# Second half of a tuned attention and swish kernel: seven products of halves in place of eight, with sums on VectorE

## The chip, the cores and the metric

The kernel runs on one core of a Trainium2 chip. The core has a matrix engine (TensorE, in the profile PE for matmuls and PEld for the loads of their weights), three engines for elementwise work (VectorE or DVE, ScalarE or ACT, GpSimd or POOL), a queue engine (SyncE or SP), a memory of 128 partitions (SBUF) and eight accumulator banks of 128 x 512 f32 (PSUM). The metric is the device time of one execution in microseconds (us).

## What is computed

Attention of two kinds of heads over 4 sequences of 768 tokens with 8 heads of 64, then, on the 3072 x 512 result, a wide layer with a gate of its own for each of its 2048 columns:

```python
def _moe_ref(x, w_in, w_out, beta) -> np.ndarray:
    h = x @ w_in
    g = h * (1.0 / (1.0 + np.exp(-beta * h)))
    return (g @ w_out).astype(np.float32)
...
    mask = np.where(retr[0, :, 0, 0, None, None], full_mask, stream_mask)
    scores = np.where(mask[None, :, :, :], scores, -1000000000.0)
    scores = scores - np.max(scores, axis=-1, keepdims=True)
    a = np.exp(scores)
    a = a / (np.sum(a, axis=-1, keepdims=True) + 1e-09)
    return np.matmul(a, v).astype(np.float32)
```

Three heads of eight see all earlier tokens (`full_mask`), five see the first 4 tokens and a window of 64 (`stream_mask`). x is 3072 x 512, w_in 512 x 2048, w_out 2048 x 512. The change is in the last product, g @ w_out, called the second part below.

## The kernel before

The tokens are cut into eight chunks of 384 (half a sequence), each of three tiles of 128 tokens. For each chunk the kernel goes through the same steps, named as its tasks are:

- `Tk`, `Tq`, `Ek`, `Eq` (chunks 0 to 2) or `Xk`, `Xq` (later chunks): keys and queries are turned so that the head dimension lies on the partitions, on PE with a copy after it or by a transposing DMA on SP. `KO`, `VO` and `lent` are small copies that put key or value blocks side by side.
- `S`, then `exp`: scores of block after block into a bank (L789), and their exponentials on ACT into the tile es (L795).
- `mask` (L820 to L835): es times a mask on DVE, in place.
- `PV` (L855), `rec`, `x` (L858, L865): es times values on PE, with a column of ones that gives the sum of each row; the reciprocal of it and the product with it on DVE.
- `Tx`, `Ex` or `Xx`: x is turned, on PE or by DMA, into xT.
- `F1`, the first part (L901): for each of 16 blocks of 128 columns of w_in four matmuls of 384 columns into a bank; `th` (L907), a tanh on ACT; `gate` (L909), (tanh + 1) times the bank, on DVE, written in bf16 to the tile gT. With tanh the gate is twice too large, and the factor 0.5 is put in at the end.
- `F2`, the second part (L924): for each tile of 128 tokens 16 matmuls of 512 columns of w_out with gT as weights; `osb` (L936, L938): the bank times 0.5 to SBUF, on ACT or DVE; `st` (L941): the store.

All instructions are recorded as tasks with dependencies, and a planner in the kernel (`Plan`) puts them in an order for every engine when the program is built: it walks through time with a cost for each task, and on PE keeps to the script `STEPS`, in which each letter is the next task of the first part (1), the second part (2) or the scores (S). `SHIFT`, `BIAS` and `FORCE` set priorities and the engine of a task, `ORDER` the order of the first loads on POOL's queue, `SESSIONS` how scores are grouped. The queues run in this order on the chip: what stands behind a waiting instruction on its engine waits too. Loads of q, k, v and the weights go through POOL's queue, transposing DMAs and stores through SP's.

Buffers are rings (`Slots`) that a task takes (`Hold`) and the last reader gives back: eight banks, two tiles gT of a whole chunk, two es tiles, three xT, two lent, four osb, five th. The first loads of chunks 0 to 2 have rings of their own (ld, qkp, qkb), unused after that.

Of the kernel before, what the change touches and what calls it, by code (L numbers as in the profile page):

```python
# [136 lines left out]
class Plan:  # L137
# [177 lines left out]
    def let_go(self, h, at):  # L315
        h.users -= 1
        h.until = max(h.until, at)
        if h.users == 0:
# [16 lines left out]
V_LAG = 8  # L335
PHASE = {3, 6}
WHOLE = set()
ADDED = set()
HEAD_PARTS = 3
SESSIONS = {1: [(4, 1), (2, 3), (3, 2), (2, 3)], 2: [(3, 2), (3, 4)], 3: [(3, 3), (4, 3), (3, 4)], 4: [(2, 3),  # L340
            (4, 3)], 5: [(3, 3), (3, 3), (4, 4)], 6: [(3, 3), (3, 3)], 7: [(3, 3), (3, 3), (4, 4)]}
# [4 lines left out]
BIAS = {"Ek": 3000.0, "Eq": -2400.0, "Ex": 2000.0, "KO": -2600.0, "KOs": 3000.0, "VO": 3000.0, "VOs":  # L346
        2600.0, "castk": -600.0, "castq": 1800.0, "exp": 2800.0, "gate": 2600.0, "mask": 2800.0, "rec":
        -2000.0, "th": 600.0, "x": -1400.0}
SHIFT = {"Ek0": 140.0, "Ek1": -170.0, "Ek2": 120.0, "Eq1": 20.0, "Eq2": 20.0, "Ex0": 120.0, "Ex1": 90.0,
# [6 lines left out]
FORCE = {"Ek0.0": "DVE", "Ek0.1": "DVE", "Ek0.2": "DVE", "Ek1.2": "ACT", "Ek2.0": "DVE", "Eq0.0": "ACT",  # L356
# [3 lines left out]
BY_PRIO = 24000.0  # L360
STEPS = ("12S12211S1111S2211S111111S1211S11211121212111121212111111111111112211122S1211222S2S2"
         "11212S222121121111112212211111S22221212111112121S12221S21111S1111121S222122212122121"
         "112112SS2121S12121111212221112111112211S22111212121122221212111222222222222222222222"
         "22")
# [3 lines left out]
def kernel(  # L368
# [46 lines left out]
    f32_r = ring(4, [128, 2, HT, D], F32, "ld", False)  # L415
    qkb = ring(6, [128, 4, HT, D], BF16, "qkb", False)
    qkp = ring(4, [128, HT, 2, D], BF16, "qkp", False)
# [6 lines left out]
    es_r = ring(2, [128, 75 * 128], BF16, "es")  # L424
    lent_r = ring(2, [128, HALF + 128], BF16, "lent")
    x_r = ring(2, [128, MO, HT, 128], BF16, "x")
    xT_r = ring(3, [128, MO, HALF], BF16, "xT")
    gT_r = ring(2, [128, FO, HALF], BF16, "gT")
    th_r = ring(5, [128, HALF], F32, "th", False)
    osb_r = ring(4, [128, d_model], F32, "osb", False)  # L430
    rec_r = ring(4, [128, HT, 2, 1], F32, "rec", False)
    w_in_sb = sb([128, MO, d_ff], BF16, "w_in_sb")
    w_out_sb = sb([128, FO, d_model], BF16, "w_out_sb")
    beta_h = sb([128, FO], F32, "beta_h")
# [6 lines left out]
    A7 = sb([128, 5, 128], BF16, "A7")  # L441
    Ac = sb([128, 5, 128], BF16, "Ac")
# [52 lines left out]
    def less(out, in_):  # L495
        nc.vector.tensor_scalar(out=out, in0=in_, scalar1=-1.0, scalar2=30000.0, op0=ALU.add, op1=ALU.mult)

    t_ac = ops("DVE", 100, [lambda: less(Ac[:, 0:3:2], Mc[:, None, :].to_broadcast([128, 2, 128]))], "adds",
               [t_mc, ops("DVE", 160, [lambda: nc.vector.memset(Ac, 0.0)], "adds", prio=-260)], prio=-240)
    t_as = ops("DVE", 100, [lambda: less(A7[:, 0:3], M7[:, 0:3]), lambda: nc.vector.tensor_copy(out=A7[:, 3:5], in_=A7[:, 1:3])], "adds", [t_m, t_ms, t_m2], prio=-240)  # L500
# [4 lines left out]
    for i, vx in enumerate(V_r.names + VO_r.names):  # L505
        t_ones[id(vx)] = ops("DVE", 24, [lambda vx=vx: nc.vector.memset(vx[:, :, :, D:DE], 1.0)], "ones", prio=-250 + i)
# [87 lines left out]
    EH = {c: Hold(es_r) for c in range(NC)}  # L594
# [75 lines left out]
    GH = {c: Hold(gT_r) for c in range(NC)}  # L670
# [73 lines left out]
    def session(c, parts, prio, lane):  # L744
# [18 lines left out]

        by_pe = c == 0 and WHERE[c][heads[0]][1] in ADDED
        add = []
        if by_pe:
            def put():
                for a, lo, part, bank in work:
                    h = part[0][0]
                    second = SIDE[c, a][0] + lo != PLACE[c, h][0]  # L770
                    m = (Ac[:, 1:4] if second else Ac[:, 0:3]) if retr[h] else (A7[:, 3:5] if second else A7[:, 0:3])
                    m = m.rearrange("p k j -> p (k j)")
                    nc.tensor.matmul(bank.buf[:, 0:m.shape[1]], ident, m, start=True, stop=False)
            add = [t_ac, t_as, t_id]

        def go(_):
            if by_pe:
                put()
            todo = []
            for s in range(2):  # L780
                at = 0
                for a, lo, part, bank in work:
                    if a == s:
                        for h, kk, i, n, place in runs_of(part):
                            todo.append((at, a, h, kk, i, n, place, bank, place + n == len(part)))
                            at += n
            for _, a, h, kk, i, n, place, bank, ends in sorted(todo, key=lambda x: x[:2]):
                of = LH[c].buf[half(a)] if kk[0][0] == "lent" else QH[c].buf[half(a), WHERE[c][h][1]]
                nc.tensor.matmul(bank.buf[:, place * 128:(place + n) * 128], kk[1](), of[:, i * 128:(i + n) * 128], start=not by_pe, stop=not by_pe or ends)  # L789
        occ = max(time) / 2.4 + 2.0 * count + (sum(time) / 2.4 + 140.0 if by_pe else 0.0)  # L790
        t = P.add(f"S{c}.{parts[0][1]}", [("PE", occ, occ + 166)], deps + add, prio, go, take=[w[3] for w in work] + [EH[c]], drop=drops, mode=64, lane=lane)
# [9 lines left out]
    def masks_and_products(c, pairs):  # L801
# [3 lines left out]
        for h in range(H):  # L805
            at, lst = PLACE[c, h]
            if c == 0 and WHERE[c][h][1] in ADDED:
                made[h] = []
                continue
# [80 lines left out]
    def first_part(c, t_beta):  # L890
        F1[c] = []
        late = []
        for fi in range(FO):
# [10 lines left out]
            if fi == HEAD_PARTS - 1 or not HEAD_PARTS:  # L904
# [5 lines left out]
                out=GH[c].buf[:, fi, :], in0=th.buf, scalar=1.0, in1=bank.buf[:, 0:HALF], op0=ALU.add, op1=ALU.mult), take=[GH[c]], drop=[bank, th])  # L910
# [188 lines left out]
```

## Time and profile before

| what | us |
|---|---|
| three runs: lowest, median, highest | 223.81, 225.12, 226.45 |
| the profiled execution, its own time | 223.37 |
| its span, from the first to the last instruction | 221.6 |
| PE busy with first part (L901, 384 columns, 512 matmuls) | 88.6 |
| PE busy with second part (L924, 512 columns, 348 records) | 82.9 |
| DVE busy with gates (L909, 128 of them) | 68.4 |
| DVE with evictions of 512 columns (L938, 13 of them) | 9.0 |
| ACT busy with tanh (L907, 128) | 73.5 |

The granted TensorE clock is 1.00 all the way. The span is what the engines' instructions take, the run's own time includes 1.8 us around it. The busy times of PE count each matmul to its modelled end, so they overlap; what one matmul costs in a row of them is read from starts. A few records are missing (348 of 368 matmuls of 512 columns are there).

### The profile page before, as it was taken

To read this page: it belongs to the slowest core of one execution; us is meant where nothing else is said; L and a number is where in the kernel's file an instruction comes from. 1 tells how busy PE (TensorE), PEld (TensorE's weight loads), DVE (VectorE), ACT (ScalarE), POOL (GpSimd) and SP (SyncE) were. 2 spreads that over 40 slices of the span, in tenths; PEclk is the share of its full clock that TensorE was granted. 3 is DMA by queue.
4 is the path that set the end of the run, shared out by engine and by line. 5 is a ranking of instruction groups with operands and counts; after the bars stand their busy time and mean duration, and the time that the engine had idled before them with its cause. 6 is when DMAs were issued, how large, how long until landed. Compare 5 with 4: busy or idle time off the path is not lost.

```text
span 221.6 us, 5127 instructions
## 1 busy us (share of the span) xinstructions
PE 213.6 (96%) x1927; PEld 125.4 (57%) x1947; DVE 147.1 (66%) x362; ACT 146.9 (66%) x283; POOL 97.7 (44%) x158
## 2 busy tenths in 40 slices
PE   7998999999999999999999999999999999999994
PEld 3665547647665545656655554655565655556553
DVE  6997866978787346568965475766856883338621
ACT  3898964669786777736867687358888886128500
POOL 8996237888598996099759600200000000000000
PEclk9999999999999999999999999999999999999999
DMA  6999999999999999979999942424012101140012
GB/s 166 167 144 206 206 190 190 187 134 211 140 145 141 123 185 193 166 106 181 155 158 144 166 71 74 114 55 133 0 44 53 39 0 47 38 155 23 3 47 96
DMA packets 95673, 26.57 MB, mean 120 GB/s; under 512 B 87184, under 2 KB 92704, under 8 KB 95648
## 3 DMA queue, kind: packets, MB, share of 16 engines
q0 software_dynamic: 66144, 13.24, 75.9%
q1 hardware_dynamic: 28784, 12.53, 27.1%
q10 hardware_dynamic: 720, 0.47, 0.7%
q8 instruction: 15, 0.25, 0.5%
q14 instruction: 10, 0.08, 0.1%
HBM read 27.27 MB, written 6.29 MB: 151 GB/s over the span
## 4 chain that ended last, share of the span: by engine, by line
PE 81%; DMA 10%; POOL 3%; DVE 2%; issue 1%; SPq 1%
PE bank L924 35%; PE bank L901 34%; DMA w_out_sb<-in_moe_w_out_dram 7%; PE bank L855 6%; PE bank L789 5%; DMA xT<-x 2%; DMA ld<-in_k_dram 2%; POOL w_in_sb L566 1%; SPq L883 1%; POOL KO L447 1%; PE bank L612 1%; POOL qkb L554 1%; PE bank L877 1%; PE bank L609 0%; DVE es L835 0%
## 5 line engine op out<-in xcount | busy, mean ns | idle before, releaser
L907 ACT ACTIVATE th<-bank,beta_h 128x384 f32<-128x384 f32 x128 | 73.5, 583 | 25.6 <-PE bank L901 19.2
L901 PE MATMUL bank<-xT,w_in_sb 128*128 128x384 bf16 x512 | 88.6, 327 | 1.0 <-ACT es L795 0.7
L924 PE MATMUL bank<-w_out_sb,gT 128*128 128x512 bf16 (+2 forms) x396 | 86.4, 363 | 1.5 <-issue 0.5
L909 DVE SCALAR_TENSOR_TENSOR gT<-th,bank 128x384 bf16<-128x384 f32 x128 | 68.4, 551 | 16.8 <-ACT th L907 10.3
L795 ACT ACTIVATE es<-bank 128x512 bf16<-128x512 f32 (+3 forms) x129 | 62.0, 587 | 20.2 <-PE bank L789 18.7
L901 PEld LDWEIGHTS <-w_in_sb 128*128 128x128 bf16 x512 | 49.2, 98 | 35.3 <-DMA w_in_sb<-in_moe_w_in_dram 1.2
L924 PEld LDWEIGHTS <-gT 128*128 128x128 bf16 x416 | 37.8, 98 | 39.1 <-issue 0.8
L835 DVE TENSOR_TENSOR es<-es,M 128x768 bf16<-128x768 bf16 (+1 forms) x35 | 18.5, 544 | 11.1 <-ACT es L795 11.1
L582 POOL DMA_DIRECT2D row<-in_k_dram x30 | 22.6, 771 | 4.1 <-DMA w_out_sb<-in_moe_w_out_dram 1.7
L938 DVE TENSOR_SCALAR osb<-bank 128x512 f32<-128x512 f32 (+2 forms) x15 | 9.7, 646 | 22.1 <-PE bank L924 21.6
L582 POOL DMA_DIRECT2D row<-in_q_dram x30 | 22.4, 785 | 0.2
L561 POOL DMA_DIRECT2D VX<-in_v_dram x24 | 21.5, 931 | 2.0 <-DMA w_in_sb<-in_moe_w_in_dram 1.7
L789 PE MATMUL bank<-QT,KT 64*128 64x128 bf16 (+2 forms) x273 | 19.4, 241 | 0.3 <-DVE QT L447 0.2
L855 PEld LDWEIGHTS <-es 128*128 128x128 bf16 x472 | 16.8, 97 | 3.7 <-DVE es L822 0.2
L855 PE MATMUL bank<-VX,es 128*128 128x65 bf16 x392 | 18.0, 193 | 0.2
L936 ACT ACTIVATE osb<-bank 128x512 f32<-128x512 f32 (+1 forms) x11 | 6.2, 568 | 18.0 <-PE bank L924 18.0
L865 DVE TENSOR_TENSOR x<-bank,rec 128x384 bf16<-128x384 f32 x32 | 17.3, 550 | 0.5
L789 PEld LDWEIGHTS <-KT 64*128 64x128 bf16 x273 | 12.8, 94 | 6.1 <-issue 4.6
L447 POOL COPY KO<-KT 128x4 bf16<-128x4 bf16 (+3 forms) x32 | 8.6, 301 | 11.6 <-PE bank L789 11.3
L789 PE MATMUL bank<-QT,KO 64*128 64x128 bf16 x80 | 11.9, 218 | 0.2 <-DVE QT L447 0.2
L447 DVE COPY VO<-VX 128x512 bf16<-128x512 bf16 (+3 forms) x12 | 5.9, 494 | 6.2 <-DMA VX<-in_v_dram 3.1
L858 DVE RECIPROCAL rec<-bank 128x6 f32<-128x6 f32 x32 | 5.9, 188 | 5.8 <-PE bank L855 5.8
(62 smaller groups left out, 108.5 us busy)
## 6 DMA issues: line engine op xcount, KB each, us to landing
out_dram<-osb SPq DMA_DIRECT2D x23, 256.0 KB, 2.6
VX<-in_v_dram POOLq DMA_DIRECT2D x24, 128.0 KB, 5.7
w_in_sb<-in_moe_w_in_dram POOLq DMA_DIRECT2D x4, 512.0 KB, 10.7
w_out_sb<-in_moe_w_out_dram POOLq DMA_DIRECT2D x4, 512.0 KB, 14.1
row<-in_k_dram POOLq DMA_DIRECT2D x30, 64.0 KB, 3.9
row<-in_q_dram POOLq DMA_DIRECT2D x30, 64.0 KB, 4.0
qkb<-in_k_dram POOLq DMA_DIRECT2D x5, 192.0 KB, 5.2
qkb<-in_q_dram POOLq DMA_DIRECT2D x5, 192.0 KB, 5.3
```

The source lines that it names most:

```text
L447: (nc.scalar.copy if e == "ACT" else eng[e].tensor_copy)(out=out, in_=in_)
L561: LD["v", c, t] = dma(f"ldv{c}.{t}", "POOL", 1000, 256, 64, list(deps) + [t_ones[id(x)] for x in V_r.names], lambda e: e.dma_start(out=VH[ ...
L582: ROW[name, c, t] = hold, [dma(f"row{name}{c}.{t}.{a}", "POOL", 750, 256, 32, [], lambda e, a=a, r=r, hold=hold, src=src: e.dma_start(out= ...
L789: nc.tensor.matmul(bank.buf[:, place * 128:(place + n) * 128], kk[1](), of[:, i * 128:(i + n) * 128], start=not by_pe, stop=not by_pe or ends)
L795: x = P.add(f"exp{c}.{a}.{lo}", [act(w * 128)], [t], prio, lambda _, e0=e0, w=w, bank=bank: nc.scalar.activation(out=EH[c].buf[:, e0 * 128 ...
L835: made[h] = [P.add(f"mask{c}.{h}", [dve(n * 128, 0.53)], list(dict.fromkeys(EXPS[c, at + i] for i in range(n))) + [t_mask], prio, lambda _ ...
L855: nc.tensor.matmul(view()[:, i, a, 0:D + 1], EH[c].buf[:, e0 * 128:(e0 + 1) * 128], val(), start=(j == 0), stop=(j == len(mine) - 1))
L865: nc.vector.tensor_mul(xo, view()[:, :, :, 0:D], rec.buf.to_broadcast([128, HT, 2, D]))
L901: nc.tensor.matmul(bank.buf[:, 0:HALF], w_in_sb[:, mo, fi * 128:(fi + 1) * 128], XTH[c].buf[:, mo, :], start=(mo == order[0]), stop=(mo == ...
L907: t = P.add(f"th{c}.{fi}", [act(HALF, 97)], [t, t_beta], c * 100, lambda _, fi=fi, bank=bank, th=th: nc.scalar.activation(out=th.buf, in_= ...
L909: GATE[c, fi] = P.add(f"gate{c}.{fi}", [dve(HALF)], [t], c * 100, lambda _, fi=fi, bank=bank, th=th: nc.vector.scalar_tensor_tensor(out=GH ...
L924: nc.tensor.matmul(bank.buf[:, 0:hi - lo], GH[c].buf[:, fi, ns * 128:(ns + 1) * 128], w_out_sb[:, fi, lo:hi], start=(fi == 0), stop=(fi == ...
```

## The change

A pair of token tiles (128 tokens each, called one and two) times w_out is seen as a product of 2 x 2 blocks: g has the rows one and two and two halves of its 2048 columns (`LOW`, `HIGH`), w_out has these halves as rows and left and right halves of 256 columns (`L`, `R`). Before, the pair takes eight block products (of 8 matmuls of 256 columns each, done as 4 x 8 of 512). Now seven block products of sums give the same result (Strassen's scheme):

- m1 = (one LOW + two HIGH) x (W[LOW,L] + W[HIGH,R]), m2 = (two LOW + two HIGH) x W[LOW,L], m3 = one LOW x (W[LOW,R] - W[HIGH,R]), m4 = two HIGH x (W[HIGH,L] - W[LOW,L]), m5 = (one LOW + one HIGH) x W[HIGH,R], m6 = (two LOW - one LOW) x (W[LOW,L] + W[LOW,R]), m7 = (one HIGH - two HIGH) x (W[HIGH,L] + W[HIGH,R]).
- The five sums of g (tasks `Ga` to `Ge`, 128 x 1024 bf16, into six tiles `sum`) are made for each pair, on DVE; `Gb`, for m2, on POOL from chunk 3 on (seven of the ten). The five sums of w_out (`W0` to `W4`, in two halves) are made once, on DVE, into `early`, the space that held the first loads, once these have been read.
- The blocks of the result are put together from the banks: `k` copies m3 and m4 from their bank to the one tile `keep` (ACT), `s` adds these two, `t` adds m1, `u` gives the two blocks m5 + m3 and m2 + m4, `w` adds the sum of m1, m3 and m4 to m7 and to m6, and `y` takes the blocks of `u` off. `s`, `t`, `u`, `w`, `y` are on DVE. Two stores follow.

Twenty of the 24 token tiles go this way: two tiles of each of the chunks 1 to 7 make a pair (seven pairs), and the third tiles of chunks 1 and 2, 3 and 4, 5 and 6 make three pairs across chunks. The three tiles of chunk 0 and the last tile of chunk 7 stay as they were (`alone`). g lies in seven slots of one tile each (`g_all`), since a tile can wait for its partner of the next chunk.

The factor 0.5 goes: the ones next to the values are 2.0, so x and h are halved, and beta is taken whole. The rings change to make room: xT two, lent one, es of 43 and 75 blocks, two output tiles of a pair each for osb. The table of additive masks, which was not used, is gone, and with it a few instructions at the start of DVE. All the numbers that set the order (`STEPS`, `SHIFT`, `BIAS`, `FORCE`, `ORDER`, `SESSIONS`, `V_LAG`, `PHASE`, `HEAD_PARTS`) are new, of which two lines are shown.

```diff
-ORDER = ["k1a", "q1a", "k1b", "q1b", "wi0", "wi1", "wi2", "wi3", "wo0", "wo1", "v10", "k2b", "v11", "v12",
-         "wo2", "q2a", "q2b", "k2a", "v20", "wo3", "v21", "v22"]
+CROSS = {1: 0, 3: 2, 5: 0}
+SUM_POOL = 'b'
+ORDER = ["q1a", "k1a", "k1b", "wi0", "wi1", "wi2", "v12", "wi3", "q1b", "wo0", "wo1", "v11", "v10", "v21",
+         "q2b", "v20", "k2b", "k2a", "q2a", "wo2", "v22", "wo3"]
...
-    gT_r = ring(2, [128, FO, HALF], BF16, "gT")
+    g_all = sb([128, 7, FO, 128], BF16, "g_all")
+    g_r = [Slots([i], True) for i in range(7)]
+    sum_r = ring(SUMS, [128, FO // 2, 128], BF16, "sum", False)
+    mid_r = ring(2, [128, 256], F32, "mid", False)
+    keep_r = ring(1, [128, 512], F32, "keep", False)
+    two_r = ring(2, [128, 2, d_model], F32, "two", False)
...
-        t_ones[id(vx)] = ops("DVE", 24, [lambda vx=vx: nc.vector.memset(vx[:, :, :, D:DE], 1.0)], "ones", prio=-250 + i)
+        t_ones[id(vx)] = ops("DVE", 24, [lambda vx=vx: nc.vector.memset(vx[:, :, :, D:DE], 2.0)], "ones", prio=-250 + i)
...
+    def weight_sums():
+
+        L, R = slice(0, 256), slice(256, 512)
+        todo = [(0, (LOW, R), (HIGH, R), ALU.subtract), (1, (HIGH, L), (LOW, L), ALU.subtract), (2, (LOW, L), (HIGH, R), ALU.add),
+                (3, (LOW, L), (LOW, R), ALU.add), (4, (HIGH, L), (HIGH, R), ALU.add)]
...
+                WSUM[n].append(P.add(f"W{n}.{i}", [dve(1024, 0.53)], [LD["wo", d] for d in deps] + READ, 150 + n, lambda e, n=n, x=x, y=y, op=op, i=i, at=at: eng[e].tensor_tensor(
+                    out=w_sum[:, n, 4 * i:4 * i + 4], in0=at(x), in1=at(y), op=op)))
...
+    def joined(one, two):
...
+        for n, x, y, op in (("a", (one, LOW), (two, HIGH), ALU.add), ("d", (two, LOW), (one, LOW), ALU.subtract), ("c", (one, LOW), (one, HIGH), ALU.add),
+                            ("b", (two, LOW), (two, HIGH), ALU.add), ("e", (one, HIGH), (two, HIGH), ALU.subtract)):
+            to = Hold(sum_r)
+            SUM[n] = to, P.add(f"G{n}{name}", [pool(1024, 2.1) if n in SUM_POOL and c > 2 else dve(1024, 0.53)], list(dict.fromkeys(gates(*x) + gates(*y))), c * 100 + 50,
+                               lambda e, x=x, y=y, op=op, to=to: eng[e].tensor_tensor(out=to.buf, in0=G(*x), in1=G(*y), op=op),
+                               take=[to], drop=[GH[z] for z in dict.fromkeys((x[0], y[0]))])
...
+            def mm(_):
+                for f in range(FH):
+                    l = of.buf[:, f] if of else g_all[:, AT[left[0]], left[1].start + f, :]
+                    r = w_sum[:, weights, f] if isinstance(weights, int) else w_out_sb[:, weights[0].start + f, weights[1]]
+                    nc.tensor.matmul(bank.buf[:, at:at + 256], l, r, start=(f == 0), stop=(f == FH - 1))
...
+        product(3, (one, LOW), 0, A, 0)
+        m4 = product(4, (two, HIGH), 1, A, 256)
+        k34 = P.add(f"k{name}", [act(512, 5)], [m4], c * 100 + 55, lambda _: nc.scalar.copy(out=keep.buf, in_=A.buf), take=[keep], drop=[A])
+        s34 = combine("s", 256, lambda e: eng[e].tensor_tensor(out=mid.buf, in0=keep.buf[:, L], in1=keep.buf[:, R], op=ALU.add), [k34], take=[mid], drop=[keep],
+                      on=pool(256, 2.1) if END_POOL else dve(256))
+        m1 = product(1, "a", 2, B, 0)
+        s134 = combine("t", 256, lambda e: eng[e].tensor_tensor(out=mid.buf, in0=B.buf[:, L], in1=mid.buf, op=ALU.add), [m1, s34], drop=[mid, B])
+        product(5, "c", (HIGH, R), E, 0)
+        m2 = product(2, "b", (LOW, L), E, 256)
+        cc = combine("u", 512, lambda e: eng[e].tensor_tensor(out=inner(), in0=E.buf, in1=keep.buf, op=ALU.add), [m2, k34], take=[to], drop=[keep, E])
+        product(7, "e", 4, F, 0)
+        m6 = product(6, "d", 3, F, 256)
+        w = combine("w", 512, lambda e: eng[e].tensor_tensor(out=outer(), in0=two_of(F.buf), in1=mid.buf[:, None, :].to_broadcast([128, 2, 256]), op=ALU.add), [m6, s134], take=[to], drop=[mid, F])
+        y = combine("y", 512, lambda e: eng[e].tensor_tensor(out=outer(), in0=outer(), in1=two_of(inner()), op=ALU.subtract), [w, cc], drop=[to],
+                    on=pool(512, 2.1) if END_POOL else dve(512))
...
+    READ += [t for t in P.tasks if t.name[:2] in ("Tk", "Tq") or t.name[:4] == "cast"]
+    weight_sums()
```

In the order, on DVE, the row L896 is the gate (L909 before), L936 a sum of g, L918 a sum of w_out, L968 the step s, L971 t, L974 u, L977 w, L978 y; on PE L888 is the first part and L952 a product. The numbers behind a name are those of its buffer.

More of the change, by code (lines that the diff above doesn't have):

```diff
@@ L493 @@
                  "masks", [t_m, t_ms, t_m2, t_mc], prio=-200)
[L495 to L500, printed above, removed]
     warm = sb([1, 1], F32, "warm")
@@ new lines, in GATE_ALL, with alone, mm @@
+    def GATE_ALL(c, fs):
+        return [GATE[c, f] for f in range(fs.start, fs.stop)]
+    def alone(c, ns, final):
+        n0 = rows_at(c, ns)
+        groups = []
+        osb = Hold(two_r)
+        for lo, hi in (((0, 256), (256, 384), (384, 512)) if final else ((0, 512),)):
+            w = hi - lo
+            bank = Hold(BANKS)
+            t = None
+            mine = []
+            for f0 in range(0, FO, 4):
+                def mm(_, f0=f0, bank=bank, lo=lo, hi=hi):
+                    for fi in range(f0, f0 + 4):
+                        nc.tensor.matmul(bank.buf[:, 0:hi - lo], g_all[:, AT[c, ns], fi, :], w_out_sb[:, fi, lo:hi],
+                                         start=(fi == 0), stop=(fi == FO - 1))
+                t = P.add(f"F2.{c}.{ns}.{f0}", [pe(w * 4, 4)], [GATE[c, fi] for fi in range(f0, f0 + 4)] + [LD["wo", f0 // 4], t],
+                          1e6, mm, take=[bank], drop=[GH[c, ns]], lane="F2")
+                mine.append(t)
+            groups.append(mine)
+            qu = "ACT" if final and lo == 256 else "SP"
+            alts = [act(w, 5), dve(w)] if not final else [act(w, 5)] if qu == "ACT" else [dve(w)]
+            e_ = P.add(f"osb{c}.{ns}", alts, [t], c * 100, lambda e, w=w, lo=lo, hi=hi, bank=bank: copy(e, osb.buf[:, 0, lo:hi], bank.buf[:, 0:w]), take=[osb], drop=[bank])
+            dma(f"st{c}.{ns}", qu, 360 if qu == "SP" else 60, 2048 if not final else 512, 8 * (w // 128 if final else 1), [e_], lambda e, lo=lo, hi=hi: e.dma_start(
+                out=out[n0:n0 + 128, lo:hi], in_=osb.buf[:, 0, lo:hi]), drop=[osb], prio=c * 10 + 15)
+        return groups
```

170 lines of the change are left out of this document (87 added, 83 removed), and 18 rows, old and new, of tables (FORCE, SHIFT).

## The prediction

> **What bounds the kernel now.** I read the page first, then the chain of waits, then the groups by form, the windows by time and the timelines. The page:
>
> ```profile
> span 221.6 us, 5127 instructions
> PE 213.6 (96%) x1927; PEld 125.4 (57%) x1947; DVE 147.1 (66%) x362; ACT 146.9 (66%) x283; POOL 97.7 (44%) x158
> PE   7998999999999999999999999999999999999994
> DVE  6997866978787346568965475766856883338621
> PE 81%; DMA 10%; POOL 3%; DVE 2%; issue 1%; SPq 1%
> ```
>
> PE is busy for 96% of the span and holds 81% of the chain. Its row of tenths shows gaps only in the first slices and at the end, so a microsecond of matmul taken out in the middle is worth nearly a microsecond, as long as nothing else fills its place. DVE is at 66%, but it reaches 9 in several slices: that is the engine that the change loads.
>
> ```profile
> 15.06 14.67 DMA w_out_sb<-in_moe_w_out_dram
> 29.77 0.39 PE bank L924
> 139.91 1.90 PE bank L855 x63
> 207.93 0.22 PE bank L924
> ```
>
> These four rows of the chain (start, length) say: the first matmul of the second part waits for the first quarter of w_out at 29.7; 63 matmuls of 65 columns, each with its own weight load, take 1.90 us, so 30 ns each; the first part's last matmul ends at 207.93.
>
> ```profile
> 204.68 4.46 DVE L909 SCALAR_TENSOR_TENSOR gT<-th,bank 128x384 bf16<-128x384 f32 x7
> 211.42 0.69 DVE L938 TENSOR_SCALAR osb<-bank 128x512 f32<-128x512 f32 x1 [2.29 <-PE bank L924]
> 214.88 0.69 DVE L938 TENSOR_SCALAR osb<-bank 128x512 f32<-128x512 f32 x1 [2.76 <-PE bank L924]
> 216.62 0.42 DVE L938 TENSOR_SCALAR osb<-bank 128x256 f32<-128x256 f32 x1 [1.05 <-PE bank L924]
> ```
>
> DVE's timeline at the end gives PE's pace, since each eviction starts when its 16 matmuls are done: 512 columns take (214.88-211.42)/16 = 216 ns, 256 columns (216.62-214.88)/16 = 109 ns. Half the columns cost half the time. The last gate ends at 209.14, 1.2 us after the last first-part matmul.
>
> **The change, part by part.**
>
> *Products.* Ten pairs of token tiles lose 32 matmuls of 512 columns each and get 7x8 = 56 of 256: 320 x 0.2163 = 69.2 us become 560 x 0.1088 = 60.9, so -8.3 us on PE, which is the path. Against the profiled execution's 223.37 us that alone would be 215.1.
>
> There is a rule against this. The Trainium skill, TensorE: Matmul & The Clock Gate, section Back-to-back issue gap, gives a sustained pace of about 131 ns for 512 columns and 81 for 128, set by matmul and weight load together. By it 320 wide matmuls would cost 42 us and 560 narrow ones at least 45, so the change would lose 3 us or more. The trace differs (216, 109 and 30 ns, above), and the sum goes by the trace.
>
> *Sums on DVE.* DVE's timeline in its densest stretch gives paces from start to start:
>
> ```profile
> 49.13 0.69 DVE L938 TENSOR_SCALAR osb<-bank 128x512 f32<-128x512 f32 x1
> 49.73 0.88 DVE L835 TENSOR_TENSOR es<-es,M 128x640 bf16<-128x640 bf16 x2
> ...
> 52.02 0.35 DVE L831 TENSOR_TENSOR es<-es,Mc 128x384 bf16<-128x384 bf16 x1
> 52.28 0.89 DVE L835 TENSOR_TENSOR es<-es,M 128x640 bf16<-128x640 bf16 x2
> ...
> 54.35 0.55 DVE L865 TENSOR_TENSOR x<-bank,rec 128x384 bf16<-128x384 f32 x1
> 54.82 0.48 DVE L835 TENSOR_TENSOR es<-es,M 128x640 bf16<-128x640 bf16 x1
> 55.22 0.55 DVE L909 SCALAR_TENSOR_TENSOR gT<-th,bank 128x384 bf16<-128x384 f32 x1
> 55.68 0.20 DVE L858 RECIPROCAL rec<-bank 128x6 f32<-128x6 f32 x1
> ```
>
> f32 512 wide: 0.60 us; f32 384: 0.46; bf16 product of two SBUF tiles 640 wide: 0.40, 384 wide: 0.26. Extended along the last two, a bf16 sum of 1024 takes 0.61; f32 256 wide, along 384 and 512, 0.33. New on DVE: 43 sums of g (7 more go to POOL) and 10 of w_out at 0.61 = 32.3; per pair u, w, y at 0.60 and s, t at 0.33, ten times: 24.6. Gone: 12 evictions of 0.60 = -7.2, and some 6 us of copies and setting up, of which ACT and POOL take a part. With 147 on the page that makes some 190. ACT gets ten copies (keep) for the eight evictions that it loses: nothing, since ACT is at 66%. What it means for PE depends on the stage:
>
> ```profile
> 50.00:60.00 10.00, 9.95 (x116) 6.82 (x114) 8.96 (x25) 9.27 (x20) 6.65 (x8) 1.00 1.73 191
> 40.00:104.00 64.00, 63.17 (x607) 37.36 (x614) 44.72 (x114) 46.07 (x89) 50.40 (x76) 1.00 1.72 159
> 104.00:208.00 104.00, 103.27 (x824) 59.00 (x833) 67.82 (x146) 71.13 (x132) 19.56 (x31) 1.00 0.61 80
> ...
> L447 DVE COPY QT<-bank 128x768 bf16<-128x768 bf16 x3 | 2.8, 949 | 0.3 <-PE bank L612 0.3
> 136.11 0.87 DVE L447 COPY KO<-KT 128x128 bf16<-128x128 bf16 x5 [1.34 <-PE bank L789]
> ```
>
> (Columns of the first three: PE, PEld, DVE, ACT, POOL busy.) From 40 to 104, chunk 1's gates to half of chunk 3's, DVE's new order has 15 sums of g and all 10 of w_out (15.3 us), 9 wide and 6 narrow combining steps (7.4), 3 masks more (1.2), 4 evictions (-2.4) and 20 copies less (-4.3: two of q and k at 0.9, the others, of keys for the most part, at 0.14, from the 0.87 us that five take in the row below): 44.7 + 17.2 = 61.9. PE has three pairs there: 63.2 - 2.5 = 60.7. So for 60 us DVE becomes as long as PE. The first fence is DVE where chunk 1's gates start, before:
>
> ```order
> L909 SCALAR_TENSOR_TENSOR gT_116<-th_118,bank_64 128x384
> L909 SCALAR_TENSOR_TENSOR gT_116<-th_119,bank_63 128x384
> L909 SCALAR_TENSOR_TENSOR gT_116<-th_120,bank_68 128x384
> L447 COPY VO_104<-VX_102 128x8x64
> L447 COPY VO_104<-VX_102 4x8x64
> L447 COPY VO_105<-VX_102 128x8x64
> L938 TENSOR_SCALAR osb_122<-bank_69 128x512
> ```
>
> and now (early is the store of the w_out sums):
>
> ```order
> L918 TENSOR_TENSOR early<-w_out_sb 128x1024 x2
> L896 SCALAR_TENSOR_TENSOR g_all<-th_113,bank_68 128x3x128
> L896 SCALAR_TENSOR_TENSOR g_all<-th_114,bank_66 128x3x128
> L896 SCALAR_TENSOR_TENSOR g_all<-th_115,bank_69 128x3x128
> L918 TENSOR_TENSOR early<-w_out_sb 128x1024 x4
> L818 TENSOR_TENSOR es_93<-es_93,Mc 128x3x128
> L896 SCALAR_TENSOR_TENSOR g_all<-th_116,bank_67 128x3x128
> ```
>
> The gates and masks of chunks 1 and 2 now queue behind sums that wait for the last quarters of w_out; ACT, then PE's banks, wait for the gates. Lower bound of the cost: 0, since a lag of DVE can be carried past 104. Upper: DVE fills no more than the 8.96 of 10 of the row at 50: 61.9/0.896 = 69.1, so 8.4 us over PE. The nearest row is the timeline above, where DVE runs from start to start without a gap while PE is busy 9.95 of 10: I take +2.0, the 1.2 of overhang and a little for waits.
>
> From 104 on, DVE's order adds 23.5 (25 sums 15.3, 16 wide and 12 narrow steps 13.6, less 6 evictions, 3 masks and some copies, 5.4): 91.3 against PE's 103.3 - 5.8 = 97.5. There it has 6.2 us of room.
>
> *Seven sums on POOL* (b, from chunk 3). A row of such a sum is not in the trace; one input of that size took
>
> ```profile
> L447 POOL COPY VO<-VX 128x1024 bf16<-128x1024 bf16 x1 | 1.0, 1036 | 3.3 <-PE bank L901 3.3
> ...
> 94.02 0.50 POOL L447 COPY lent<-QT 64x384 bf16<-64x384 bf16 x1 [6.56 <-DMA QT<-row]
> 94.58 0.75 POOL L447 COPY VO<-VX 128x512 bf16<-128x512 bf16 x1
> ...
> 94.09 1.59 DVE L835 TENSOR_TENSOR es<-es,M 128x640 bf16<-128x640 bf16 x2
> ...
> 58.00 2.55 POOL L447 COPY VO<-VX 128x1024 bf16<-128x1024 bf16 x2 [3.29 <-PE bank L901]
> ...
> 58.68 1.01 DVE L909 SCALAR_TENSOR_TENSOR gT<-th,bank 128x384 bf16<-128x384 f32 x2
> ```
>
> so with two inputs between 1.04 and 2.1. The next three are a collision: two masks on DVE took 1.59 us beside POOL's copies and 0.88 without (at 49.73), so 0.71 lost; two gates, with one input in SBUF, took 1.01 beside a copy of POOL, 0.5 each as elsewhere. The Trainium skill, SBUF — State Buffer, section Who interferes with whom, says that a VectorE instruction with two SBUF inputs and a GpSimd one that reads SBUF exclude each other for the whole instruction; the trace agrees, and sums of g are of this kind. The place where it costs most is the end. DVE's last rows, before:
>
> ```order
> L909 SCALAR_TENSOR_TENSOR gT_116<-th_119,bank_67 128x384
> L938 TENSOR_SCALAR osb_123<-bank_68 128x512
> L938 TENSOR_SCALAR osb_124<-bank_64 128x512
> L938 TENSOR_SCALAR osb_125<-bank_70 128x256
> L938 TENSOR_SCALAR osb_123<-bank_63 128x128
> ```
>
> and now, from the last gate on:
>
> ```order
> L896 SCALAR_TENSOR_TENSOR g_all<-th_114,bank_65 128x3x128
> L977 TENSOR_TENSOR two_111<-bank_63,mid_107 128x2x256
> L936 TENSOR_TENSOR sum_102<-g_all 128x1024
> L936 TENSOR_TENSOR sum_105<-g_all 128x1024
> L936 TENSOR_TENSOR sum_104<-g_all 128x1024
> L968 TENSOR_TENSOR mid_108<-keep_109 128x256
> ```
>
> while POOL's last rows, which before were copies, are
>
> ```order
> L456 COPY VO_92<-VX_89 4x24x64
> L936 TENSOR_TENSOR sum_102<-g_all 128x1024 x2
> L936 TENSOR_TENSOR sum_105<-g_all 128x1024
> L936 TENSOR_TENSOR sum_101<-g_all 128x1024
> ```
>
> So behind the last gate there now stand a combining step and three sums, and beside them a sum on POOL. PE's first product that needs a sum (a, sum_102) now comes 24 narrow matmuls, 2.6 us, after the last first-part one. The sum is there after 1.2 + 0.6 + 0.6 = 2.4: no wait. If POOL's sum_101 takes the memory first, it is 1.04 to 2.1 later, a wait of 0.8 to 1.9; I take +1.2. The other six come 4 us or more of PE work ahead of their products: 0 to begin with, the room of DVE covers them.
>
> *The start.* In POOL's queue one V tile of 128 KB now stands ahead of the first quarter of w_out (and one V more and two q or k ahead of the third). At the rate of
>
> ```profile
> 20.00:30.00 10.00, 9.81 (x69) 5.61 (x68) 8.22 (x18) 8.82 (x19) 2.66 (x4) 1.00 1.24 207
> ```
>
> 207 GB/s a V tile is 0.6 us, on the chain at 29.7: +0.6 (0 if PE's session that is now ahead of it covers that, 1.5 with the third quarter).
>
> *At nothing:* the new constants (2.0 in the ones, no 0.5 at the output) change no instruction's length; xT rings of two and one lent tile are written a chunk after their last reader, behind 10 us of first part; stores go two at a time on SP behind the same transposes, with two output buffers a pair apart (6 us of products); ACT's copy to the one keep tile waits for step u of the pair before, with exps and tanhs queued behind it, but u comes some three products earlier; w_out sums are due some 10 us later. If the tail grew they would show as waits on DMA.
>
> Sum: 223.37 - 8.3 + 0.6 + 2.0 + 1.2 = 218.9. The profiled execution lies below all three runs shown (223.81 to 226.45, median 225.12); the same difference from the median is 220.6. I forecast 219.8, between them.
>
> **The rivals.** *Full gain:* the stretch to 104 and the lock cost nothing; 3.2 less, 216.6. For it: PE was never held at a DVE share of 8.96. Against: the overhang. *DVE becomes the bound* in that stretch at 0.896: 6.4 more, 226.2. For it: 61.9 against 60.7, and waits on two sides. Against: its banks let a lag pass. *The lock decides, slower than before:* POOL's seven sums stop DVE for all of their length, 7 x 2.1 = 14.7 against 6.2 of room, so 8.5 instead of 1.2: 227.1. It turns the change into a loss from 1.8 us a sum ((6.2+6.5)/7). For it: the 1.59. Against: the gates' 1.01, and DVE has two-input work for only part of that time. *No gain from fewer columns:* a floor per matmul, as the page's rule would have it: 3 us or more over before, 228; against it stand 109 and 30 ns.
>
> **How the numbers follow.** Forecast (217.5 to 222.8) 0.52; full gain 0.17; DVE bound 0.16; lock 0.12; floor 0.03. A measurement of this kernel can tell about 1% from no change: below 222.9 is faster, above 227.4 slower. Faster: 0.52 + 0.17 and a little of DVE bound, 0.70; within 1%: the rest of it and half of the lock, 0.20; slower 0.10. The range 215.5 to 226.5 leaves out most of the lock and the floor, some 0.16.
>
> **What would show it.** PE: 560 matmuls of 256 at a pace of 109 ns, busy time some 8 us lower; another pace breaks the first term. DVE busy near 190 us, its share at 40 to 104 over 9.3 of 10; PE waiting there for gates, masks or sums shows the second. A sum on POOL beside DVE sums of 1 to 2 us instead of 0.7 shows the lock; PE waiting for sum_102 at the end its price. The first second-part matmul at 30 us shows the start.

## The result, and the profile after

| | us |
|---|---|
| before, median (lowest to highest) | 224.47 (223.44 to 226.45) |
| after, median of 4 runs (lowest to highest) | 235.07 (233.04 to 238.19) |
| ratio after to before, 95% interval | 1.0431 [1.0314, 1.0549] |
| forecast | 219.8, range 215.5 to 226.5 |

The kernel became slower by 4%, and the time lies outside the range. The profiled execution of the kernel after is its slowest one, 238.19 us; where that matters, the text says so. The ratios here and below leave out executions more than 1.5% above the fastest of the same kernel (in e1 one of 353.6 us, in e6 five of ten); the medians hold all.

The page of the kernel after (the engines' busy time, the rows of tenths of PE, DVE and POOL, the granted clock in tenths, the chain's shares):

```profile
span 236.4 us, 5719 instructions
PE 214.6 (91%) x2180; PEld 151.0 (64%) x2180; DVE 196.7 (83%) x425; ACT 147.7 (62%) x291; POOL 128.1 (54%) x183
PE   7888999998999989979967977999999997999894
DVE  5993968799999699979559977888999997948972
POOL 8996457699599999279939990140012021300300
PEclk9997999999999999999989995899999999999999
PE 53%; DVE 24%; POOL 10%; DMA 7%; issue 2%; ACT 2%; SPq 0%; ACTq 0%; DVEq 0%; POOLq 0%
```

PE holds 53% of the chain in place of 81%, DVE 24% in place of 2%. PE's row of tenths, which had no gap in the middle, has 6 and 7 in the slices from 118 to 148 us, and the clock's row, which was full before, falls to 5 there.

What PE waited for, in total us, times, longest, says by whom it was held:

```profile
PE bank L888 <- DVE g_all L896: 5.2, 5, 2.2
PE bank L842 <- DVE es L822: 3.2, 2, 3.0
PE bank L952 <- DVE sum L936: 2.5, 3, 1.5
PE bank L888 <- DMA xT<-x: 1.3, 1, 1.3
...
PE bank L952 <- DVE two L977: 1.2, 1, 1.2
```

Before, no wait of PE after the start was over 0.3 us. All but one of these waits are for DVE: for a gate, a mask, a sum, a combining step. DVE is 83% busy, so its total does not tell why; the groups do. Sums of g on DVE and on POOL:

```profile
L936 DVE TENSOR_TENSOR sum<-g_all 128x1024 bf16<-128x1024 bf16 x43 | 41.0, 980 | 3.9 <-PE bank L952 3.8
L936 POOL TENSOR_TENSOR sum<-g_all 128x1024 bf16<-128x1024 bf16 x7 | 15.8, 2284 | 56.5 <-DVE g_all L896 50.7
```

A sum on POOL takes 2.28 us; a sum on DVE 0.98 on the mean. The next rows are the two engines' timelines at the longest stall, POOL's row first:

```profile
137.83 4.30 POOL L936 TENSOR_TENSOR sum<-g_all 128x1024 bf16<-128x1024 bf16 x2
...
135.97 0.68 DVE L936 TENSOR_TENSOR sum<-g_all 128x1024 bf16<-128x1024 bf16 x1
136.58 0.68 DVE L974 TENSOR_TENSOR two<-bank,keep 128x512 f32<-128x512 f32 x1
138.50 4.19 DVE L936 TENSOR_TENSOR sum<-g_all 128x1024 bf16<-128x1024 bf16 x1 [1.25 <-PE bank L952]
142.61 0.55 DVE L822 TENSOR_TENSOR es<-es,M 128x768 bf16<-128x768 bf16 x1
```

Alone a sum takes 0.68 us on DVE. The one at 138.50 falls into two sums on POOL, back to back from 137.83 to 142.13, and ends 0.56 us after the second: 4.19 us. Behind it in DVE's queue is a mask (L822), and PE's attention product waits for that mask:

```profile
143.22 0.24 PE L842 MATMUL bank<-VO,es 128*128 128x65 bf16 x1 [3.01 <-DVE es L822]
```

The clock behind it, in windows of 2 us (busy time of PE, PEld, DVE, ACT, POOL, then the clock; the last two columns are DMA):

```profile
142.00:144.00 2.00, 0.79 (x13) 0.79 (x14) 2.00 (x5) 0.00 (x0) 0.13 (x1) 0.57 0.00 0
144.00:146.00 2.00, 2.00 (x13) 1.38 (x11) 1.43 (x5) 0.20 (x1) 0.00 (x0) 0.50 0.25 92
146.00:148.00 2.00, 2.00 (x11) 1.44 (x10) 0.92 (x2) 0.39 (x1) 0.00 (x0) 0.50 0.45 170
148.00:150.00 2.00, 2.00 (x25) 1.22 (x24) 1.32 (x5) 0.47 (x1) 0.00 (x0) 0.72 0.00 0
```

After the stall of 3 us PE is busy all the time, at half of its clock, until 149. So one DVE instruction that was held for 3.5 us cost 3 us of waiting and, in this execution, about 3 us more of slow matmuls (5.9 us at half clock, from 143.2 to 149.1).

### The profile page after: what moved, and what is told of

Same layout as the page of the kernel before. It is cut to its first block, busy times and chain, and to the rows that moved or that the text cites. A ratio compares the mean times of both kernels' runs of the same rounds, so it can differ in the third digit from the quotient of the medians.

```text
span 236.4 us, 5719 instructions
## 1 busy us (share of the span) xinstructions
PE 214.6 (91%) x2180; PEld 151.0 (64%) x2180; DVE 196.7 (83%) x425; ACT 147.7 (62%) x291; POOL 128.1 (54%) x183
## 4 chain that ended last, share of the span: by engine, by line
PE 53%; DVE 24%; POOL 10%; DMA 7%; issue 2%; ACT 2%; SPq 0%; ACTq 0%; DVEq 0%; POOLq 0%
PE bank L888 21%; PE bank L952 19%; DVE sum L936 11%; PE bank L842 5%; DVE g_all L896 5%; POOL row L585 5%; PE bank L779 4%; PE bank L1001 4%; DMA early<-in_k_dram 3%; POOL KO L456 3%; DMA VX<-in_v_dram 3%; DVE es L822 2%; DVE x L852 2%; DMA row<-in_q_dram 1%; POOL VO L456 1%
## 5 line engine op out<-in xcount | busy, mean ns | idle before, releaser
L888 PE MATMUL bank<-xT,w_in_sb 128*128 128x384 bf16 x512 | 91.9, 333 | 6.7 <-DVE g_all L896 5.2
L888 PEld LDWEIGHTS <-w_in_sb 128*128 128x128 bf16 x512 | 49.8, 100 | 38.9 <-issue 10.0
L896 DVE SCALAR_TENSOR_TENSOR g_all<-th,bank 128x384 bf16<-128x384 f32 x128 | 64.8, 547 | 8.2 <-ACT th L894 5.8
L936 POOL TENSOR_TENSOR sum<-g_all 128x1024 bf16<-128x1024 bf16 x7 | 15.8, 2284 | 56.5 <-DVE g_all L896 50.7
L952 PEld LDWEIGHTS <-sum 128*128 128x128 bf16 x400 | 39.1, 100 | 10.2 <-DVE sum L936 3.4
L936 DVE TENSOR_TENSOR sum<-g_all 128x1024 bf16<-128x1024 bf16 x43 | 41.0, 980 | 3.9 <-PE bank L952 3.8
L952 PE MATMUL bank<-early,sum 128*128 128x256 bf16 x240 | 30.9, 278 | 2.5 <-DVE sum L936 2.5
L952 PE MATMUL bank<-early,g_all 128*128 128x256 bf16 x160 | 20.6, 280 | 1.2 <-DVE two L977 1.2
L456 POOL COPY KO<-KT 128x128 bf16<-128x128 bf16 (+3 forms) x49 | 19.7, 437 | 3.4 <-ACT KT L456 3.0
L822 DVE TENSOR_TENSOR es<-es,M 128x768 bf16<-128x768 bf16 (+1 forms) x35 | 18.0, 527 | 3.4 <-ACT es L785 3.2
L952 PE MATMUL bank<-w_out_sb,sum 128*128 128x256 bf16 x160 | 20.6, 280 | 0.0
L952 PEld LDWEIGHTS <-g_all 128*128 128x128 bf16 x160 | 15.7, 100 | 4.0 <-issue 1.2
L967 ACT COPY keep<-bank 128x512 f32<-128x512 f32 x10 | 5.8, 584 | 19.5 <-PE bank L952 15.2
```

The lines of the kernel that those rows point to most:

```text
L456: (nc.scalar.copy if e == "ACT" else eng[e].tensor_copy)(out=out, in_=in_)
L822: made[h] = [P.add(f"mask{c}.{h}", [dve(n * 128, 0.53)], list(dict.fromkeys(EXPS[c, at + i] for i in range(n))) + [t_mask], prio, lambda _ ...
L888: nc.tensor.matmul(bank.buf[:, 0:HALF], w_in_sb[:, mo, fi * 128:(fi + 1) * 128], XTH[c].buf[:, mo, :], start=(mo == order[0]), stop=(mo == ...
L896: GATE[c, fi] = P.add(f"gate{c}.{fi}", [dve(HALF)], [t], c * 100, lambda _, fi=fi, bank=bank, th=th: nc.vector.scalar_tensor_tensor(out=g_ ...
L936: lambda e, x=x, y=y, op=op, to=to: eng[e].tensor_tensor(out=to.buf, in0=G(*x), in1=G(*y), op=op),
L952: nc.tensor.matmul(bank.buf[:, at:at + 256], l, r, start=(f == 0), stop=(f == FH - 1))
```

## The experiments

**e1, the kernel after again,** on the chip of e2 to e8 (e9 to e12 ran on another one, where the kernel before took 223.76 us against 223.95 and 224.06).

> The changed kernel once more, unchanged, as the base that the other runs of this group are read against. All theories: 232 to 236 us, kernel before 224 to 225.

236.96 us median, 236.55 for the three executions that the ratio holds; ratio 1.0558 [1.0498, 1.0617]. No trace of it is read.

**e2, the seven sums b on VectorE,** the recorded order otherwise the same row for row:

```diff
-   lambda e, x=x, y=y, op=op, to=to: eng[e].tensor_tensor(out=to.buf, in0=G(*x), in1=G(*y), op=op),
+   lambda e, x=x, y=y, op=op, to=to: nc.vector.tensor_tensor(out=to.buf, in0=G(*x), in1=G(*y), op=op),
```

> The seven sums b run on VectorE at the place in the recorded order where GpSimd had them; every other instruction keeps its place. Theory lock (GpSimd's sums of 2.1 us stop VectorE's own sums, and the stalls of TensorE that follow are drawn out by a lower clock): sums on VectorE fall back to 0.68 us each, the waits at 122, 128, 138, 197 and 225 us shrink, 224 to 229. Theory load (VectorE has too much work whoever blocks it): 4.3 us more on VectorE, 234 to 238. Theory queue (GpSimd's loads come late because of its 128 us of work): 15.8 us less on GpSimd, 229 to 232.

226.69 us, ratio 1.0159 [1.0082, 1.0236]: 9.9 us less than e1's 236.55 (8.9 by the two ratios), though DVE has seven sums more to do. The group of sums, now fifty:

```profile
L936 DVE TENSOR_TENSOR sum<-g_all 128x1024 bf16<-128x1024 bf16 x50 | 34.1, 712 | 1.8 <-PE bank L952 1.7
```

Fifty take 34.1 us where 43 took 41.0. What follows: most of the loss hangs on these seven instructions being GpSimd's. Whether because GpSimd's result is late or because VectorE is held, this run does not tell; e9 does.

**e3, the seven sums left out,** and **e4, all fifty sums left out** (the products then read constant weights, and the output is not the layer's). The instructions of these sums are gone, and the products get other weights; the line of e4, which e3 has for the seven alone:

```diff
...
-   l = of.buf[:, f] if of else g_all[:, AT[left[0]], left[1].start + f, :]
+   l = w_in_sb[:, 0, f * 128:(f + 1) * 128] if of else of.buf[:, f] if of else g_all[:, AT[left[0]], left[1].start + f, :]
```

> The seven sums b of GpSimd are left out; their products take a block of w_in as weights, so the output is not the layer's. Order otherwise as in the changed kernel. Theory lock: 223 to 228, at or a little below the run with b on VectorE. Theory load: 232 to 235, since VectorE's own work is the same. Theory queue: as with b on VectorE, 229 to 232. The difference to the run with b on VectorE is the price of seven plain sums there, 0 to 4.3 us.

> All 50 sums of g are left out, on VectorE and GpSimd; the products that took them have a block of w_in as weights, so the output is not the layer's. VectorE loses 26 us of plain work and its blocked time. Theories lock and load: 217 to 221, the seven products show their gain, less a start that is 2.4 us later than before. Theory queue, or a cause in the combining steps: 224 or more.

e3 took 224.31 us, ratio 1.0015 [0.9983, 1.0048]; e4 222.71 us, ratio 0.9893 [0.9813, 0.9973]. So seven sums cost 2.4 us where DVE does them, and all fifty 4.0. e4 lies between the ranges of all its theories: even without one sum the kernel was only 1% under before (0.6% by the medians), not the 3.7% that the 8.3 us of the products alone would be. Something else held PE, and e4's gaps of PE show one place; below the gap, DVE's row just ahead of it:

```profile
118.25 3.73 PE L888 MATMUL bank<-xT,w_in_sb 128*128 128x384 bf16 x12 [2.68 <-DVE g_all L896]
...
117.44 0.29 DVE L456 COPY VO<-VX 128x512 bf16<-128x512 bf16 x1 [6.09 <-DMA VX<-in_v_dram]
117.65 3.80 DVE L896 SCALAR_TENSOR_TENSOR g_all<-th,bank 128x384 bf16<-128x384 f32 x8
```

A copy of values for chunk 6 stands in DVE's queue ahead of eight gates, and waits 6.1 us for its load; PE runs out of free banks. In the kernel after the same copy waits 5.65 us, and PE 2.25.

**e5, e6, e7** start from e2, since it has no sums on GpSimd, and **e8** from the kernel after. e5 adds 60 matmuls of zeros at four places of the start, e6 gives that copy of values to GpSimd, e7 does both, e8 lets the planner order everything anew with the sums on VectorE at 0.63 ns an element. The edit of e7, which holds those of e5 and e6:

```diff
+    WARM_UP = {'S0.20': 12, 'Tk1.2': 20, 'PV0.3': 16, 'Tx0.3': 12}
     for t in P.run(key, AHEAD):
+        if t.name == "VO6":
+            t.engine = "POOL"
+        for _ in range(WARM_UP.get(t.name, 0)):
+            nc.tensor.matmul(t.take[0].buf[:, 0:128], zeros[:, 0:128], zeros[:, 0:128], start=True, stop=True)
+        WARM_UP.pop(t.name, 0)
         t.emit(t.engine)
```

> As e2_b_on_vector (all sums on VectorE; 226.69 us in its runs), with 60 matmuls of zeros added on TensorE at four places of the start where it idled in the earlier profiles (ahead of the last score task of chunk 0, of the transposes of chunk 1's second half of keys, of the last attention products of chunk 0 and of the last transpose of x). The product is otherwise the same. Theory (the granted clock falls to about half for some microseconds after TensorE has idled in the start, and that is what the start costs beyond the idle time): the granted clock stays at 1.0 from 10 to 25 us (it was 0.79 in 15-20 and 0.87 in 20-25, that is 1.7 us of work lost) and the time falls by 1 to 2 us, to about 225. Rival (the start waits for loads and the clock costs nothing there, since TensorE would wait anyway): the clock is 1.0 but the time stays within 0.5 us of 226.7. Second rival (the clock falls for another reason than idling): the clock still falls.

> As e2_b_on_vector, with one copy of values (VO of chunk 6, 128x512) moved from VectorE's queue, where it stood ahead of gates while its load had not landed (5.8 us of idle VectorE at 117 to 123), to GpSimd's queue, at the same place of the order. The product is the same. Theory (that in-order wait is the 2.4 us stall of TensorE at 121 to 124, and the clock of 0.87 and 0.79 in 120 to 130 follows from it): the stall is gone, the clock there is 1.0, the time falls by 3 to 4 us to about 223. Rival (TensorE is short of other work there, so it waits for the next thing): the stall moves and less than 1 us is gained.

> e5_filled_start and e6_value_copy together (all sums on VectorE, zeros matmuls in the start, the copy of values on GpSimd). The product is the same. If start and stall are separate causes, their gains add: about 221 to 222 us, 1% under the kernel before. If they share a limit (loads), it is about 223 to 224, no better than the better of the two.

> The kernel after with the planner told that all fifty sums are VectorE's, at 0.63 ns for each of their 1024 elements in place of 0.53, so that it orders every engine for them; its tables are otherwise as in the change. The product is the same. Theory (the loss is the lock and single in-order waits, not that the order was searched for wrong prices): it lands where e2_b_on_vector does, 225 to 229. Rival (an order that knows the real place and price of the sums repairs the rest by itself): under 223.

| | median us | ratio to before, 95% interval |
|---|---|---|
| e5, filled start | 226.64 | 1.0118 [1.0073, 1.0164] |
| e6, copy of values on GpSimd | 223.53 | 0.9904 [0.9875, 0.9933] |
| e7, both | 224.90 | 1.0022 [0.9989, 1.0055] |
| e8, planned anew | 224.40 | 1.0007 [0.9973, 1.0040] |

The kernel before took 224.06 us beside these. e6 did as expected: 3.2 us under e2. Its ratio rests on the five executions of 221.1 to 222.6 us, though; by the median of all ten it is 0.2% under before. Its DVE at that place has no idle row any more, and the five sums there take 0.62 us each:

```profile
112.49 3.10 DVE L896 SCALAR_TENSOR_TENSOR g_all<-th,bank 128x384 bf16<-128x384 f32 x5
115.63 3.10 DVE L936 TENSOR_TENSOR sum<-g_all 128x1024 bf16<-128x1024 bf16 x5
118.65 3.33 DVE L896 SCALAR_TENSOR_TENSOR g_all<-th,bank 128x384 bf16<-128x384 f32 x7
```

e5 kept the clock at 1.00 from 10 to 25 us and gained nothing, as the first rival had it, by which PE waits for loads there whatever its clock. With e6's copy moved, the filling even cost 1.4 us (e7 to e6), so that e7 lies above both of its forecasts. e8 lands between e2 and e6, by 2.3 us under e2: the order planned for the real place of the sums repairs a part, so that the theory's 225 to 229 was too high, but the rival's 223 isn't reached either. Its longest wait of PE is 2.2 us, for a transpose of x.

**e9, sums on GpSimd that nobody reads.** All fifty sums on VectorE as in e2; GpSimd adds the same halves at the same seven places into a buffer that nobody reads any more:

```diff
+        def both(e, to, x, y, op):
+            if e == "POOL":
+                for i in range(0, FH, 4):
+                    nc.gpsimd.tensor_tensor(out=zeros.rearrange("p (f j) -> p f j", f=4), in0=x[:, i:i + 4], in1=y[:, i:i + 4], op=op)
+            nc.vector.tensor_tensor(out=to, in0=x, in1=y, op=op)
...
```

> As e2_b_on_vector (all fifty sums on VectorE, 226.69 us), but GpSimd also adds the same halves at the seven places where the kernel after has it do so, in two instructions of 512 each time, into a buffer that nobody reads any more. Nothing waits for GpSimd's result; what is written to the output is unchanged. Theory (what the sums on GpSimd cost is that they hold up VectorE's work beside them): the time goes back most of the way to the kernel after, 232 to 238 us, and VectorE's sums beside GpSimd's take 1.5 us or more in place of 0.68. Rival (the cost was that TensorE or VectorE waited for GpSimd's slow results of 2.1 us): 226 to 228, as without them.

234.26 us (233.87 to 234.66), ratio 1.0472 [1.0447, 1.0498]: most of the loss is back, 7.6 us over e2 (7.0 by the ratios), with nobody waiting for GpSimd's results. That GpSimd, as busy again as in the kernel after, asks for its loads later is not what PE pays for: its waits for DMA total 2.5 us in this trace and 4.9 in e2's, its waits for gates 6.3 and 2.3. VectorE is held. Three instructions of DVE beside four half sums on GpSimd (POOL's row first):

```profile
135.21 5.99 POOL L936 TENSOR_TENSOR zeros<-g_all 128x512 bf16<-128x512 bf16 x4
...
137.59 1.18 DVE L937 TENSOR_TENSOR sum<-g_all 128x1024 bf16<-128x1024 bf16 x1 [0.38 <-PE bank L958]
138.69 1.50 DVE L822 TENSOR_TENSOR es<-es,M 128x768 bf16<-128x768 bf16 x1
140.12 1.64 DVE L937 TENSOR_TENSOR sum<-g_all 128x1024 bf16<-128x1024 bf16 x1
...
144.28 0.68 DVE L937 TENSOR_TENSOR sum<-g_all 128x1024 bf16<-128x1024 bf16 x1
```

The mask (0.55 us alone) takes 1.50, a sum 1.64, and POOL's half sums 1.5 each where the shortest of the fourteen takes 1.15: each engine waits for the other. Once POOL has ended, at 141.20, the next sum takes 0.68 again.

**e10, e11, e12** start from e6. e10 puts 28 matmuls of zeros ahead of chunk 3's first part, where PE waits 1.4 us for xT; e11 makes chunk 3's transposes of x on TensorE (`XT_PE = {0, 1, 2, 3}` in place of `{0, 1, 2}`); e12 is e6 unchanged.

> As e6_value_copy, with 28 matmuls of zeros (128 columns each, some 1.5 us) on TensorE ahead of chunk 3's first task of the first part, whose last quarter of xT lands 1.4 us late at 104 us. The product is the same. Theory (the granted clock falls in some executions after that wait, and those executions are the ones of 224.6 us against 221.4 us at full clock): no execution shows a mean clock under 0.99, and all are at 221 to 222, if the filling itself costs nothing beside the wait. Rival (the clock falls for reasons other than this wait): the two groups of times stay.

> As e6_value_copy, with chunk 3's transposes of x on TensorE (12 transposes, about 1 us, and four evictions on VectorE or ScalarE) in place of four DMA transposes in SP's queue, and the order planned again with that. The product is the same. Theory (the wait of 1.4 us at 104 us comes from SP's queue, where the transposes of x stand behind those of the next chunk's queries): the wait is gone, 219.5 to 221.5 us and fewer executions with a lowered clock. Rival (the added work on a full VectorE takes the place of the wait): 222 or more.

> e6_value_copy again, unchanged, as the measure for e10_filled_wait and to narrow its interval against the kernel before: 223.5 us median in two groups, 221.4 at a mean clock of 1.0 and 224.6 at 0.985 to 0.992; ratio 0.99.

e10: 224.00 us, ratio 0.9905 [0.9878, 0.9932] (the ratio holds four of seven executions; the median of all is 0.1% above before's 223.76), inconclusive. The zeros ran ahead of the task, but the wait lies inside it, before its last quarter, and stayed (2.3 us in the profiled execution, whose start was late); three executions at a clock of 0.997 to 1.0 took 221.3 to 221.9 us, four at 0.984 to 0.990 took 224.0 to 227.3. e11: 230.99 us, ratio 1.0329 [1.0283, 1.0374], a miss. The wait at 104 us is gone, but the planner moved other transposes with it: two of chunk 4's now stand behind two of the next queries on SP, and PE waits 3.8 us for them at 126. e12: 222.89 us, ratio 0.9929 [0.9897, 0.9962]. The ratios of e6 and e12 make this version 0.7 to 1.0% faster than before, but they leave out eight of its 22 executions, all at a mean clock of 0.977 to 0.992 (the kernel before beside them has four of 41 at 0.99, all kept in its mean). By the medians of all, the gain is 0.2 to 0.4%. It is the best version found that computes the layer.

## Why the prediction was wrong

**Products, -8.3: right in the pace.** A product of eight matmuls in a row takes 0.87 us from start to start, 109 ns each, as forecast. How much of it arrived can be read in e6, where the clock was at 1.00 in the profiled execution:

```profile
PE 207.7 (94%) x2180; PEld 148.3 (67%) x2180; DVE 190.0 (86%) x431; ACT 148.2 (67%) x291; POOL 112.2 (51%) x177
```

PE's busy time is 5.9 us lower than before, not 8.3; where the other 2.4 us are was not found. (An estimate for a part: the trace before lacks 20 records of 512 columns, and each leaves a hole of some 0.05 us, two paces of 0.216 less a length of 0.38, which counts as idle.) The rule on a floor per matmul is excluded by the pace.

**The start, +0.6 (0 to 1.5): right in size.** PE is idle 4.0 us in the first 20 against 2.9 before, 1.1 more. But the first second-part matmul, which was to come at 30 us, came at 32.2, 2.4 later than before, and one V tile of 0.6 us doesn't explain that; the script of PE had first-part work there, so little of it was lost.

**DVE from 40 to 104 us, +2.0 (0 to 8.4): about right.** In e6 the windows give DVE 59.8 us (forecast 61.9) and PE 60.1, 3.9 us idle against 0.8 before: 3.1 us, of which 1.4 is the wait for xT at 104, which is SP's queue and no DVE work.

**The seven sums on POOL, +1.2: this step failed.** Its price of one sum (1.04 to 2.1) was near: 2.12 to 2.62, 2.28 on the mean. At the end the wait was even as drawn:

```profile
222.33 2.12 POOL L936 TENSOR_TENSOR sum<-g_all 128x1024 bf16<-128x1024 bf16 x1 [18.40 <-DVE g_all L896]
...
222.71 3.50 DVE L936 TENSOR_TENSOR sum<-g_all 128x1024 bf16<-128x1024 bf16 x3
...
225.06 1.05 PE L952 MATMUL bank<-early,sum 128*128 128x256 bf16 x8 [1.45 <-DVE sum L936]
```

Wrong was the sentence "The other six come 4 us or more of PE work ahead of their products: 0 to begin with, the room of DVE covers them". It looked at who waits for the sum on POOL, and nobody did. It should have looked at who stands behind the instruction of DVE that is held: the queue is in order, and gates and masks stand there, which PE needs at once. 6.2 us of room over 104 us cannot be spent at one place. PE's waits for DVE at five places that the sums touch (127.9, 143.2, 181 and 186, 197.2, 225.1) make 8.0 us in the kernel after, and 0.6 in e2; with the 3 us of lost work behind the stall at 143 this makes 10.4 us, near the 9.9 between e1 and e2. That it is so near is in part luck: e2's trace has falls of the clock of its own, at other places, and 2.9 us more of waits for loads, so the two traces' spans differ by 8.1 only. The rival of the lock had the mechanism and a price of 8.5 us; it stood at 0.12, on the ground that gates beside a copy on POOL were not slower. They are not, here either (e6's seven gates in 3.33 us, above, run beside copies on POOL), but sums and masks are of the other kind.

The Trainium skill, SBUF — State Buffer, section SBUF: two separate sides, states that of a GpSimd instruction and a VectorE one with two SBUF inputs the one that starts first gets the shared pair of ports for its whole instruction, and the other blocks. The rows at 138.50 agree: the sum on DVE passed neither before nor between two sums on POOL that follow each other. In e9's rows the two engines alternated, with 1.2 to 1.6 us for each of DVE's; what decides between the two is not shown.

**A wait that was not in the prediction: +3.2.** The copy of values at the head of DVE's queue (e2 to e6: 3.2 us; to e12, on the other chip, 3.8). The prediction had counted the loads of values only at the start. Three rows of the kernel after, two of POOL and one of DVE, show it:

```profile
101.79 0.50 POOL L456 COPY lent<-QT 64x384 bf16<-64x384 bf16 x1 [5.69 <-DMA QT<-row]
...
113.74 2.72 POOL L564 DMA_DIRECT2D VX<-in_v_dram  x3
...
121.02 0.29 DVE L456 COPY VO<-VX 128x512 bf16<-128x512 bf16 x1 [5.65 <-DMA VX<-in_v_dram]
```

A copy of queries holds POOL's queue until 101.8 (before, until 94.0), so the values are asked for at 113.7 (before, at 105.5). Before, the copy of these values stood on POOL, where it held up nothing that PE needed; now it stood on DVE ahead of gates.

**The clock, which was not in the prediction.** It was 1.00 all through the profile before, and was taken for a constant.

So of the 15.3 us between forecast and result 8 to 9 are the lock (8.9 to 9.9, less the 1.2 that were counted), 3.2 the copy of values; the remaining 3 to 4 us are spread over PE's busy time, the wait for xT and the clock, and no run divides them. (The lock was measured where the kernel after took 236.55 us, 1.5 more than in the result.)

## What to carry to other kernels

An engine with room in its total still has a queue in order: of work that is put on GpSimd, ask first which VectorE instructions read two SBUF tiles in that time, then what stands behind them and who waits for that. A price for a held instruction goes up to the whole of the other engine's instruction (e9's mask lost 0.95 us beside half sums of 1.5), and here to both where two followed each other (3.5 us beside 4.3). Offloading seven sums of 0.6 us to save 4 us of VectorE cost 9 to 10; the same sums on VectorE, with one late copy out of its way, made the change worth 0.2 to 0.4% over all executions.

## What the runs showed of the hardware

- The granted clock of TensorE falls after short stalls, and in steps of one length. In the kernel after it is 0.50 from 19.4 to 22.8 us, from 121.8 to 125.2 and from 142.3 to 149.1 (read in windows of half a microsecond), behind waits of 0.93 and 0.69 us, of 2.25, and of 3.0. These falls last 3.4, 3.4 and 6.8 us, and begin 30 times and 6 times 3.41 us apart. The fourteen falls in the traces of e2 to e5, e7 and e9 to e11 last 3.4 us too, one of them 6.8. In the 3.4 us ahead of a fall PE was busy for 0 to 0.67 of the time (0.53, 0.35 and 0.39 in the kernel after). It does not fall each time: e8 shows 1.00 in spite of waits of 2.2 and 1.7 us, e9 behind a stretch of 3.4 us with PE busy for 0.48 of it. How a wait lies to these stretches may decide; no run tests it. The Trainium skill, TensorE: Matmul & The Clock Gate, Part 1, gives a window of 3.4 us that runs freely, two states, full and half, and a fall after an idle window. The two levels and the window agree; that a window in which PE was busy for half of the time is enough does not.
- What such a fall is worth: of e6's ten executions the five at a mean clock of 0.999 to 1.0 took 221.1 to 222.6 us, the five at 0.985 to 0.992 224.5 to 225.1. In e12, the same kernel, the two groups meet: 220.4 to 222.9 at 0.998 to 1.0, 222.9 to 226.6 at 0.977 to 0.992. How much of these 2 to 3 us is slow matmuls and how much the waits that came with them, no kept trace shows. Filling the start with matmuls of zeros kept the clock up there and saved nothing (e5), which suggests that a fall costs only where PE is the bound afterwards.
- Two sums on GpSimd back to back held one VectorE sum for 4.19 us in place of 0.68, and unread half sums took 1.5 us in place of 1.15 themselves: the exclusion works both ways.
